# Two recurrent attention layers with streamed weights: at most three weight transfers under way, held back by a one-word read on SyncE

## The chip, the cores and the metric

The kernel runs on one core of a Trainium2 chip. The metric is the device time of one execution in microseconds, from the first to the last instruction. A core has five engines with a program each: TensorE (PE, matmuls; its weight loads are listed apart as PEld), VectorE (DVE), ScalarE (ACT), GpSimd (POOL) and SyncE (SP, which here only issues transfers). Sixteen DMA engines move data between device memory and the on-chip buffer. An engine waits for another one, or for a transfer, by a semaphore.

## The reference

Four layers follow each other, A B A B, each with a layer norm before it and a residual sum after it. The change touches layer A alone: attention over segments of 32 rows, each with 8 rows of memory that the segment before it has produced.

```python
# one A layer: x (2048, 640), 32 heads of 192, 64 segments of 32 rows, 8 memory rows
mem = mem0
for s in range(64):
    h = concat([mem, x[32*s : 32*s+32]])          # 40 rows
    q, k, v = h @ Wq, h @ Wk, h @ Wv              # 640 -> 32 x 192 = 6144 each
    p = softmax(where(mask, q k^T / sqrt(192), -1e9))
    o = (p v) @ Wo                                # 6144 -> 640
    mem = o[:8]                                   # the next segment needs it
    outs.append(o[8:])
```

Each segment needs the one before it, so the 64 segments of a layer are a chain, and each uses all four weight matrices. Layer B (a linear attention with softmax features) isn't touched.

## The kernel before

The four matrices of layer A are 31 MB together in bf16. Most of them stays in the on-chip buffer; the rest is loaded again in every segment. The heads are taken in four rounds r = 0, 1, 2, 3 of 8 heads, and every other segment goes through them backwards, so that the round that ends one segment begins the next. Rounds 1 and 2 are resident. Of rounds 0 and 3, which change places, 10 pieces of Wq, Wk and Wv (3 + 3 + 4 "slots" of 128 x 1536) and the four quarters of Wo's 128 x 7680 piece (`wo_end`) are streamed: as soon as TensorE has read a slot in the first round of a segment (n = 0), the piece of the last round (n = 3) is loaded into it.

```python
SLOTS = {"Q": 3, "K": 3, "V": 4}
...
def load_slot(m, r, b):                 # 128 x 1536 bf16 = 384 KB
    if holds.get((m, b)) != r:
        holds[m, b] = r
        nc.sync.dma_start(out=slot[m, b][:], in_=wview[m][:, b, PW * r:PW * r + PW])
...
def load_wo(r, into=None):              # four transfers of 480 KB
    t = into if into is not None else wo_end[:, :] if r in (0, 3) else wo_mid[:, 7680 * (r - 1):7680 * r]
    for k in range(4):
        nc.sync.dma_start(out=t[:, 1920 * k:1920 * k + 1920].rearrange("p (c m) -> p c m", m=640),
                          in_=wov[:, 12 * r + 3 * k:12 * r + 3 * k + 3, :])
```

The chain, cut to the order of its steps. The order of instructions on each engine is the order of the program here.

```python
def project(hT, ps, m, n, s, steps):
    ...
    for i in steps:
        b = (i + KC - ns) % KC if n == 0 else i      # round 0 of a segment reads the slots first
        w = piece(m, r, b)
        for g in range(4):
            ... nc.tensor.matmul(o[32 * g:32 * g + 32, 0:384], lhsT=hT[:, b, :], rhs=rhs, ...)   # L681
        if n == 0 and b >= KC - ns:
            load_slot(m, order[NR - 1], b)           # L522, on SyncE
...
for s in range(NSEG):
    for n, r in enumerate(order):
        ... project Q (with scores, softmax sums and normalisation of round 0 in between when n == 1)
        ... project K, project V
        if n > 0:
            O, OT = attend(E, n - 1)                 # L733
            extra_v(s, n + 1)                        # GpSimd: 2 x 14 KB, V of the segment's last 8 rows
        if n > 0:
            S, E = weigh()                           # L715, L722, L764
            wo_round(W, order[n - 1], OT, range(4), n == 1, False)        # L751
            sums(S, E)                               # L779
            wo_round(W, order[n - 1], OT, range(4, 12), n == 1, False)
            if n == 1:
                load_wo(order[NR - 1])               # L535, on SyncE: wo_end has been read
        ...
            next_kq(s, n)                            # GpSimd: copies K and Q of the segment's last 8 rows into
                                                     # place (L658 to L661), loads 96 KB of the next (kqb, L653)
    keep_busy(idle, 4)                               # matmuls whose result isn't used
    O, OT = attend(E, NR - 1)
    keep_busy(idle, 2)
    wo_round(W, order[NR - 1], OT, range(12), False, True)                # reads the new wo_end
    keep_busy(idle, 3)
    ... W -> wt -> hT[:, :, 0:8]                     # L866, L867: memory rows of the next segment
```

The chain projects the 8 memory rows and the first 24 rows of a segment; Q, K and V of its last 8 rows were computed before the chain and are read from device memory. In what follows a segment starts with the copy L867 (hT<-wt), with which its memory rows are complete.

The probes of the change use nothing of this but the order on SyncE, which has no other work in the chain.

Of the kernel before, what the change touches and what calls it, by code (L numbers as in the profile page):

```python
# [9 lines left out]
BF16 = mybir.dt.bfloat16  # L10
# [90 lines left out]
class Kernel:  # L101
# [389 lines left out]
    def layer_A(self, xn_dram, at_dram, li):  # L491
        nc, tc = self.nc, self.tc
        KC, NSEG = self.KC, self.NSEG
        dram = self.dram
        NR = 4
        PW = 1536
        self.kqb_d = dram.tile([NSEG, P, NR, 192], BF16, name=f"kqb{li}")
        self.vb_d = dram.tile([NSEG, NR, 2, 8, 896], BF16, name=f"vb{li}")
        self.otb_d = dram.tile([NSEG, P, 384], BF16, name=f"otb{li}")
        wview = self.wview  # L500
        wov = self.A_Wo.rearrange("h d m -> (h d) m").rearrange("(c p) m -> p c m", p=P)
        with tc.tile_pool(name=f"A{li}_wres", bufs=1) as wres:


            NRES = sum(KC - (SLOTS[m] if r in (0, 3) else 0) for m in "KQV" for r in range(NR))
            big = wres.tile([P, NRES * PW], BF16, name="w_res")
            res, at = {}, 0
            for r in (3, 0, 1, 2):
                for m in "KQV":
                    for b in range(KC - (SLOTS[m] if r in (0, 3) else 0)):  # L510
                        res[m, r, b] = big[:, at * PW:at * PW + PW]
                        at += 1
            slot = {(m, b): wres.tile([P, PW], BF16, name=f"wslot{m}{b}") for m in "KQV" for b in range(KC - SLOTS[m], KC)}
            holds = {}
            wo_mid = wres.tile([P, 24 * 640], BF16, name="wo_mid")
            wo_end = wres.tile([P, 12 * 640], BF16, name="wo_end")
            unread = set(res)

            def load_slot(m, r, b):
                if holds.get((m, b)) != r:  # L520
                    holds[m, b] = r
                    nc.sync.dma_start(out=slot[m, b][:], in_=wview[m][:, b, PW * r:PW * r + PW])  # L522

            def load_matrix(m, r):
                for b in range(KC):
                    if (m, r, b) in unread:
                        unread.remove((m, r, b))
                        nc.sync.dma_start(out=res[m, r, b], in_=wview[m][:, b, PW * r:PW * r + PW])
                    elif (m, r, b) not in res:
                        load_slot(m, r, b)  # L530

            def load_wo(r, into=None):
                t = into if into is not None else wo_end[:, :] if r in (0, 3) else wo_mid[:, 7680 * (r - 1):7680 * r]
                for k in range(4):
                    nc.sync.dma_start(out=t[:, 1920 * k:1920 * k + 1920].rearrange("p (c m) -> p c m", m=640),  # L535
                                      in_=wov[:, 12 * r + 3 * k:12 * r + 3 * k + 3, :])

            def piece(m, r, b):
                assert (m, r, b) in res or holds[m, b] == r
                return res[m, r, b] if (m, r, b) in res else slot[m, b]  # L540

            self.A_pre(xn_dram, li, load_matrix, piece, wo_mid, wo_end)
            self.A_chain(xn_dram, at_dram, li, load_slot, piece, load_wo, wo_mid, wo_end, big)
            self.A_post(at_dram, li, wo_mid, wo_end, big)

# [68 lines left out]
    def A_chain(self, xn_dram, at_dram, li, load_slot, piece, load_wo, wo_mid, wo_end, big):  # L614
        nc, tc, KC, NSEG = self.nc, self.tc, self.KC, self.NSEG
        scale = float(self.Dh) ** -0.5
        NR = 4
        with tc.tile_pool(name=f"A{li}_ch", bufs=1) as sp, \
# [16 lines left out]
            def rounds(s):  # L635
                return range(NR) if s % 2 == 0 else range(NR - 1, -1, -1)
# [31 lines left out]
            def project(hT, ps, m, n, s, steps):  # L668
                order = rounds(s)
                r = order[n]  # L670
                ns = SLOTS[m]
                for i in steps:
                    b = (i + KC - ns) % KC if n == 0 else i
                    w = piece(m, r, b)
                    for g in range(4):
                        if m == "V":
                            rhs = w[:, 384 * g:384 * g + 384]
                        else:
                            rhs = w[:, :].rearrange("p (c j) -> p c j", j=P)[:, :, 32 * g:32 * g + 32]
                        o = ps[g % 2] if m == "V" else ps  # L680
                        nc.tensor.matmul(o[32 * g:32 * g + 32, 0:384], lhsT=hT[:, b, :], rhs=rhs, start=(i == 0),  # L681
                                         stop=(i == KC - 1), tile_position=(0, 32 * g), skip_group_check=True)
                    if n == 0 and b >= KC - ns:
                        load_slot(m, order[NR - 1], b)

            def keys_or_queries(hT, m, n, s):
                ps = pqp.tile([P, 512], F32, name="ps_qk", tag="qk")
                project(hT, ps, m, n, s, range(KC))
                return ps
# [71 lines left out]
            def weigh():  # L761
                S = scores()
                E = sp.tile([P, 160], BF16, name="E", tag="E")
                nc.scalar.activation(out=E[:], in_=S[:, 0:160], func=ACT.Exp, scale=scale)  # L764
                return S, E
# [12 lines left out]
            def sums(S, E):  # L778
                nc.tensor.matmul(S[:, 256:416], lhsT=self.ones_blk[:, :], rhs=E[:, :], start=True, stop=True,  # L779
                                 skip_group_check=True)  # L780
# [18 lines left out]
            for s in range(NSEG):  # L799
# [3 lines left out]
                order = rounds(s)  # L803
                for n, r in enumerate(order):
                    pq = pqp.tile([P, 512], F32, name="ps_qk", tag="qk")
                    project(hT, pq, "Q", n, s, range(2))
                    if n == 1:
                        S, E = weigh()
                        next_kq(s, 0)
                    project(hT, pq, "Q", n, s, range(2, 4))  # L810
                    if n == 1:
                        sums(S, E)
                        normalise(S, E)
                    project(hT, pq, "Q", n, s, range(4, KC))
                    to_rows(pq, "Q")
                    pk = keys_or_queries(hT, "K", n, s)
                    to_rows(pk, "K")
                    if n == 0 and s > 0:
                        nc.gpsimd.dma_start(out=self.otb_d[s - 1], in_=otb[:, :, :, :].rearrange("p r c t -> p (r c t)"))
                        if s % 2 == 0:  # L820
                            store_rows(s - 2, ob_old)
                    pv = [pop.tile([P, 512], F32, name=f"ps_v{x}", tag=f"v{x}") for x in range(2)]
                    project(hT, pv, "V", n, s, range(3))
                    if n > 0:
                        O, OT = attend(E, n - 1)
                        if n + 1 < NR:
                            extra_v(s, n + 1)
                        elif s + 1 < NSEG:
                            extra_v(s + 1, 0)
                        if n == 1:  # L830
                            otb = sp.tile([P, NR, 12, 8], BF16, name="otb", tag="otb")
                        attend_rest(O, OT, otb, order[n - 1])
                    project(hT, pv, "V", n, s, range(3, KC))
                    if n > 0:
                        S, E = weigh()
                        wo_round(W, order[n - 1], OT, range(4), n == 1, False)
                        sums(S, E)
                        wo_round(W, order[n - 1], OT, range(4, 12), n == 1, False)
                        if n == 1:
                            load_wo(order[NR - 1])  # L840
                        if s == NSEG - 1 and n == 2:
                            load_wo(3, big[:, 0:7680])
                    v_rows(pv, n, 0, 0)
                    v_rows(pv, n, 1, 0)
                    v_rows(pv, n, 0, 1)
                    if n > 0:
                        normalise(S, E)
                    v_rows(pv, n, 1, 1)
                    if n > 0:
                        next_kq(s, n)  # L850
                    if n == NR - 1 and s + 1 < NSEG:
                        hT = hx_transpose(s + 1)
                        if s % 2 == 0 and s + 2 < NSEG:
                            load_rows(s + 2)
# [79 lines left out]
```

The softmax here doesn't subtract the row's maximum and nothing guards it: scores larger than these inputs give would overflow.

## Time and profile before

| what | value |
|---|---|
| time, median of 3 runs | 4346.16 us (4339.44 to 4354.84) |
| span of the profiled execution | 4350.8 us |
| TensorE busy | 3683.1 us, 85% |
| VectorE, ScalarE, GpSimd busy | 52%, 47%, 41% |
| mean granted TensorE clock | 0.948 |
| bytes moved | 983.28 MB, 226 GB/s over the span |
| of these by SyncE's and ScalarE's loads, q1 and q10 | 861.74 and 49.36 MB |
| q0 (transfers issued by GpSimd) | 60.56 MB |
| q8 and q14, "instruction" | 9.98 and 1.65 MB |

How to read it. The page gives the busy time of each engine, then the span in 40 slices with tenths of busy time, then the DMA queues, the chain of work that ended last, the costliest groups of instructions and the issues of transfers. Groups are written as line, engine, operation, tiles (out<-in), count. A wait is written as who waited, on which line, for whom: total us, how often, the longest. "Issue" stands for time in which an engine waited for nothing that the profile shows. Timeline rows begin with the start in us from the span's start and the length; rows of stretches give the length, then the busy time of PE, PEld, DVE, ACT and POOL with the number of instructions, the granted clock, the DMA share and GB/s. The page has two stretches of layer A's chain, at 272 to 1819 us and 2443 to 3976 us from the second segment on, two of layer B, and before each chain a short one in which the last 8 rows of every segment, whose projections don't depend on the chain, are projected for all segments at once.

### The profile page before, as it was taken

How to read it: one execution, taken by the hardware profiler on the slowest of the kernel's cores; microseconds unless marked ns; L12 is line 12 of the kernel's file. 1: busy time of each engine (PE TensorE's matmuls, PEld its weight loads, DVE VectorE, ACT ScalarE, POOL GpSimd, SP SyncE). 2: the span in 40 equal slices, each digit the busy share in tenths (PEclk: the TensorE clock that was granted, in tenths of full speed). 3: DMA queues.
4: the chain of work that ended last, by engine and by line, in shares of the span. 5: the costliest groups of instructions: out<-in, count | busy, mean ns of one | idle time of the engine just before them, and what ended most of it. 6: DMA issues, size and time to landing. Idle time of an engine off the chain costs nothing. (4 is left out here: it accounts for less than half of the span.)

```text
span 4350.8 us, 181511 instructions
## 1 busy us (share of the span) xinstructions
PE 3683.1 (85%) x77592; PEld 2223.0 (51%) x77608; DVE 2248.2 (52%) x5570; ACT 2024.4 (47%) x4973; POOL 1800.7 (41%) x5269
## 2 busy tenths in 40 slices
PE   5888888888888888869869888888888888888698
PEld 4645555555555555535347455555555555555353
DVE  4245555555555555536732455555555555554464
ACT  1245555555555555525412455555555555555152
POOL 1035555555555555430000355555555555553300
PEclk9989999999999999979989899999999999999798
DMA  7777777677677677740076876777777777777200
GB/s 258 214 264 271 254 274 259 247 268 257 247 261 262 239 275 258 273 126 1 31 248 193 280 269 240 273 259 258 276 250 271 251 262 271 252 266 272 84 1 25
DMA packets 613364, 983.28 MB, mean 226 GB/s; under 512 B 145098, under 2 KB 424650, under 8 KB 612554
## 3 DMA queue, kind: packets, MB, share of 16 engines
q1 hardware_dynamic: 459498, 861.74, 54.5%
q0 software_dynamic: 68224, 60.56, 4.6%
q10 hardware_dynamic: 84832, 49.36, 4.1%
q8 instruction: 609, 9.98, 0.9%
q14 instruction: 201, 1.65, 0.1%
HBM read 903.16 MB, written 68.16 MB: 223 GB/s over the span
## 5 line engine op out<-in xcount | busy, mean ns | idle before, releaser
L681 PEld LDWEIGHTS <-hT 128*32 128x32 bf16 x30720 | 785.9, 98 | 596.4 <-issue 217.7
L681 PE MATMUL ps_qk<-w_res,hT 128*32 128x384 bf16 x14336 | 804.8, 334 | 51.0 <-issue 48.0
L666 POOL DMA_DIRECT2D Vp<-vb x1024 | 539.1, 531 | 593.3 <-PE ps_o L733 518.5
L693 ACT ACTIVATE raw<-ps_qk 128x384 bf16<-128x384 f32 x1024 | 501.9, 490 | 547.4 <-PE ps_qk L681 529.4
L707 DVE CAST Vp<-ps_v 32x384 bf16<-32x384 f32 x1024 | 552.7, 540 | 36.3 <-PE ps_v L681 26.9
L751 PEld LDWEIGHTS <-OT 128*32 128x32 bf16 x24576 | 437.1, 99 | 234.0 <-issue 101.3
L698 DVE STREAM_TRANSPOSE QT<-raw 128x256 bf16<-128x256 bf16 x512 | 228.1, 445 | 613.9 <-ACT raw L693 604.1
L709 ACT ACTIVATE Vp<-ps_v 32x384 bf16<-32x384 f32 x1024 | 494.4, 483 | 64.0 <-PE ps_v L681 43.7
L658 POOL COPY QT<-kqb 128x64 bf16<-128x64 bf16 x512 | 121.8, 238 | 838.9 <-PE ps_s L722 403.5
L681 PE MATMUL ps_v<-w_res,hT 128*32 128x384 bf16 x6144 | 407.0, 330 | 29.7 <-issue 27.2
L786 DVE TENSOR_TENSOR E<-E,ps_s 128x160 bf16<-128x160 bf16 x512 | 164.6, 322 | 485.4 <-ACT ps_s L785 485.4
L751 PE MATMUL ps_w<-wo_mid,OT 128*32 128x160 bf16 x12288 | 351.1, 250 | 65.6 <-issue 63.0
L695 DVE STREAM_TRANSPOSE KT<-raw 128x384 bf16<-128x384 bf16 x512 | 296.1, 578 | 71.8 <-ACT raw L693 57.3
L739 ACT ACTIVATE OT<-ps_o 128x240 bf16<-128x240 f32 x512 | 190.0, 371 | 287.8 <-PE ps_o L733 275.7
L764 ACT ACTIVATE E<-ps_s 128x160 bf16<-128x160 f32 x512 | 155.7, 304 | 360.8 <-PE ps_s L722 356.6
L751 PE MATMUL ps_w<-wo_end,OT 128*32 128x160 bf16 x12288 | 290.5, 235 | 30.2 <-issue 15.9
L722 PE MATMUL ps_s<-QT,KT 128*40 128x40 bf16 (+1 forms) x6144 | 183.4, 189 | 127.9 <-DVE KT L695 63.3
L758 PE MATMUL ps_idle<-wo_mid,ident 128*128 128x384 bf16 x1152 | 270.0, 346 | 0.0
L681 PE MATMUL ps_v<-wslotV,hT 128*32 128x384 bf16 x4096 | 249.6, 332 | 22.8 <-issue 20.7
L743 DVE CAST OT<-ps_o 128x240 bf16<-128x240 f32 x512 | 195.9, 383 | 126.6 <-PE ps_o L733 122.9
L745 POOL COPY otb<-OT 128x48 bf16<-128x48 bf16 x1024 | 198.4, 231 | 125.1 <-ACT OT L739 117.3
L653 POOL DMA_DIRECT2D kqb<-kqb x256 | 148.0, 578 | 232.5 <-DMA vb<-wo_end 153.9
(148 smaller groups left out, 5485.4 us busy)
## 6 DMA issues: line engine op xcount, KB each, us to landing
wo_end<-in_A_Wo_dram SPq DMA_DIRECT2D x520, 480.0 KB
wslotV<-in_A_Wv_dram SPq DMA_DIRECT2D x536, 384.0 KB
wslotK<-in_A_Wk_dram SPq DMA_DIRECT2D x402, 384.0 KB
wslotQ<-in_A_Wq_dram SPq DMA_DIRECT2D x402, 384.0 KB
kqb<-wo_mid ACTq DMA_DIRECT2D x16, 1536.0 KB
kqb<-kqb POOLq DMA_DIRECT2D x256, 96.0 KB, 5.5
Vp<-vb POOLq DMA_DIRECT2D x1024, 14.0 KB, 4.8
vb<-wo_end ACTq DMA_DIRECT2D x128, 112.0 KB
```

Of the source, the lines that this page charges most:

```text
L666: nc.gpsimd.dma_start(out=Vs[n % 2][64 * G + 32:64 * G + 40, :], in_=self.vb_d[s, r, G])
L681: nc.tensor.matmul(o[32 * g:32 * g + 32, 0:384], lhsT=hT[:, b, :], rhs=rhs, start=(i == 0), stop=(i == KC - 1), tile_position=(0, 32 * g), ...
L693: nc.scalar.activation(out=raw[:], in_=ps[:, 0:384], func=ACT.Copy)
L695: nc.vector.transpose(out=KT[:, :, 0:32], in_=raw[:, :].rearrange("p (c j) -> p c j", j=32))
L698: nc.vector.transpose(out=qv[:, :, 0:4:3, 8:40], in_=rv[:, :, 0:3:2, :])
L707: nc.vector.tensor_copy(out=o, in_=i)
L709: nc.scalar.activation(out=o, in_=i, func=ACT.Copy)
L739: nc.scalar.activation(out=OT[0].rearrange("p c q -> p (c q)"), in_=O[0][:, 0:240], func=ACT.Copy)
L743: nc.vector.tensor_copy(out=OT[1].rearrange("p c q -> p (c q)"), in_=O[1][:, 0:240])
L745: nc.gpsimd.tensor_copy(out=otb[:, r, 6 * G:6 * G + 6, :], in_=OT[G][:, :, 0:8])
L751: nc.tensor.matmul(W[32 * g:32 * g + 32, 0:160], lhsT=OT[c // 6][:, c % 6, 8:40], rhs=w[:, 640 * c + 160 * g:640 * c + 160 * g + 160], sta ...
L758: nc.tensor.matmul(ps[:, 0:384], lhsT=self.ident[:, :], rhs=wo_mid[:, 0:384], start=True, stop=True, skip_group_check=True)
```

## The change

Layer A gets a pacing of the streamed weights. `flying` lists the last loads. Before a fourth one, SyncE issues a probe: a transfer of one word (two bf16 values) out of the buffer that the third last load fills, into a scratch tensor in device memory. The probe reads what that load writes, so it has to wait until the load has landed, and since SyncE issues in order, the next load stands behind it. So no more than three streamed loads are under way. It is meant to keep the DMA queues short, so that other users of the DMA engines wait less. The ten slots and the four quarters of `wo_end` in each segment are paced; the loads before the chain and one of the last segment into `w_res` are not. The scratch tensor has 16 rows, used in turn.

```diff
+            probe = dram.tile([16, 2], BF16, name=f"probe{li}")
+            flying = []
+            probes = [0]
+
+            def pace(ap):
+                if len(flying) == 3:
+                    nc.sync.dma_start(out=probe[probes[0] % 16:probes[0] % 16 + 1, :], in_=flying.pop(0)[0:1, 0:2])
+                    probes[0] += 1
+                flying.append(ap)
+
-            def load_slot(m, r, b):
+            def load_slot(m, r, b, paced=False):
                 if holds.get((m, b)) != r:
                     holds[m, b] = r
+                    if paced:
+                        pace(slot[m, b])
                     nc.sync.dma_start(out=slot[m, b][:], in_=wview[m][:, b, PW * r:PW * r + PW])
...
-            def load_wo(r, into=None):
+            def load_wo(r, into=None, paced=False):
                 t = into if into is not None else wo_end[:, :] if r in (0, 3) else wo_mid[:, 7680 * (r - 1):7680 * r]
                 for k in range(4):
+                    if paced:
+                        pace(t[:, 1920 * k:1920 * k + 1920])
                     nc.sync.dma_start(out=t[:, 1920 * k:1920 * k + 1920].rearrange("p (c m) -> p c m", m=640),
...
-                        load_slot(m, order[NR - 1], b)
+                        load_slot(m, order[NR - 1], b, True)
...
-                            load_wo(order[NR - 1])
+                            load_wo(order[NR - 1], None, True)
```

A transfer that is issued on SyncE takes one of eight semaphores in turn, and each has to be free again. In the changed program loads and probes alternate, so a probe also waits for the probe four before it.

## The prediction

> **What bounds the kernel now.** I read the page from the top: shares of busy time, the 40 slices, the DMA queues. The two "A" layers fill most of the span (slices 2 to 17 and 22 to 37), and in them TensorE is at 8 tenths and the DMA at 7, with no engine full:
>
> ```profile
> PE 3683.1 (85%) x77592; PEld 2223.0 (51%) x77608; DVE 2248.2 (52%) x5570; ACT 2024.4 (47%) x4973; POOL 1800.7 (41%) x5269
> ...
> PE   5888888888888888869869888888888888888698
> ...
> q1 hardware_dynamic: 459498, 861.74, 54.5%
> ...
> q8 instruction: 609, 9.98, 0.9%
> ```
>
> Two lines carry what follows. q1 holds the weight stream. q8 is TensorE's own program: 77592 + 77608 = 155200 instructions in 609 packets are 255 for each packet, and 9.98 MB / 155200 is 64 bytes each.
>
> So I asked what TensorE's matmuls wait for in the chain of the first A layer (272.6 to 1819.4 us, 62 whole segments). The waits, in us, times and the longest:
>
> ```profile
> PE ps_qk L681 <- issue: 43.0, 35, 2.2
> PE ps_w L751 <- issue: 37.8, 32, 1.7
> PE ps_s L722 <- DVE KT L695: 30.0, 124, 0.3
> PE ps_v L681 <- issue: 25.6, 17, 2.2
> PE ps_o L733 <- issue: 14.1, 11, 2.2
> PE ps_s L722 <- POOL KT L661: 13.9, 19, 2.8
> PE ps_s L722 <- issue: 9.3, 8, 1.5
> ```
>
> "Issue" means that no semaphore held it. With two waits of L715 (4.1) that is 133.9 us here and 122.7 us in the other chain: **257 us** in which TensorE has data and no instruction. The timeline of TensorE shows one such wait, and the one before it:
>
> ```profile
> 879.24 0.73 PE L751 MATMUL ps_w<-wo_mid,OT 128*32 128x160 bf16 x31 [0.80 <-issue]
> ...
> 883.36 0.32 PE L751 MATMUL ps_w<-wo_mid,OT 128*32 128x160 bf16 x7
> 885.32 0.37 PE L751 MATMUL ps_w<-wo_mid,OT 128*32 128x160 bf16 x9 [1.64 <-issue]
> ```
>
> Between the two starts lie 127 matmuls and 128 weight loads, 255 instructions: one packet of q8. The packet itself ran at 883.09, 3.85 us after 879.24, and TensorE went on 2.23 us after its start. In the trace 215 of the packets in the two chains are followed by such a stop, 270 us together, restart at a median 2.38 us after the packet's start. All of them lie 6 to 20 us after a segment's start. The stretches of one segment say why:
>
> ```profile
> 841.30:845.30 4.00, 3.74 (x90) 2.22 (x89) 2.30 (x7) 2.31 (x6) 0.78 (x2) 1.00 0.70 205
> ...
> 849.30:853.30 4.00, 3.61 (x105) 2.18 (x101) 1.89 (x6) 2.52 (x6) 1.09 (x4) 1.00 1.03 400
> 853.30:857.30 4.00, 3.01 (x98) 1.90 (x91) 2.05 (x5) 2.20 (x6) 3.03 (x12) 1.00 1.05 383
> ...
> 861.30:865.10 3.80, 3.71 (x106) 2.25 (x105) 1.63 (x5) 1.76 (x5) 3.02 (x10) 1.00 0.10 16
> ```
>
> The last two columns are DMA share and GB/s. The DMA is full from about 845 to 859 and empty at the end; TensorE's busy time (first column after the length) is worst where it is full. From the first use of a block to the start of the next block's packet the trace has a median of 1.1 us at 20 to 22 us of a segment (empty queue) and 3.7 to 3.8 us at 10 to 14 us (about 5 to 6 us of stream queued). Blocks take 4.4 to 5.3 us to execute; a delay plus 2.4 us above that is a stop. So the limit to stay under is a delay of about 2.0 to 2.4 us.
>
> **What the Trainium skill says.** "Runtime: NRT & Kernel Launch", section "Instruction fetch mechanics", says that a sequencer fetches its program over a DMA queue of its own, in 16 KiB blocks of 256 instructions, mostly hidden. The block size agrees (9.98 MB / 609); hidden it is not here. "DMA: Bandwidth & Descriptors", section "Queues, rings and completion order", has each DMA engine go round between queues by packets; a fetch thus does not wait for the whole backlog, which agrees with a delay that stops growing at 3.8 us. The section "Anatomy of one DMA" of that page puts some 2 us of fixed time on a transfer, mostly the receipt. The trace agrees: the segment's first load is issued at 841.92 and its first engine reports at 844.66, 2.74 us, of which 1.05 us is movement (393 KB at 375 GB/s). "TensorE: Matmul & The Clock Gate", Part 1, says that an idle window puts the array to half clock for about 3.4 us. The trace has such stretches in 51 of 124 whole segments, mostly beside a stop of over 1 us; those segments last 25.70 us on average, the others 24.24.
>
> **The change, part by part.** There are 128 segments, on average 24.84 us. Each streams 10 slots of 393 KB and 4 pieces of Wo of 491 KB, 5.9 MB.
>
> *Adds:* 14 probes a segment, one descriptor of 4 bytes each, behind two loads at most. SyncE's small stores (attn<-obB) take 0.26 us each; 14 x 0.26 = 3.7 us of SyncE in 24.8, which has only these loads to do. Nothing is added on TensorE, VectorE, ScalarE or GpSimd.
>
> *Takes away:* the backlog. Now all ten slots are issued within 5.3 us of the first (0.63 to 5.9 us into a segment, medians of the trace) and Wo follows at 8.0 to 10.7. With three under way, of which one is always being set up or waiting for its receipt (2.74 - 1.05 = 1.7 us), one to one and a half transfers stand in the queue, 1.0 to 1.6 us. The empty-queue delay of 1.1 us plus this is 2.1 to 2.7 us at worst and mostly below 2.4. I take it that four fifths of the 257 us go: 205 us. With the long stops go some of the half-clock stretches: 51 x (25.70 - 24.24) = 74 us, of which I count half, 37. The wait for the kqb rows (POOL KT L661, 13.9 + 11.9 = 26 us) shrinks for the same reason; half is 13. Sum: **255 us**, 2.0 us a segment.
>
> *Moves:* the arrivals, later. The loop is: third-last landing, probe, load, landing. That is 2.74 us, some 0.45 us for another packet on the slowest engine, 0.26 us probe and 0.2 us of gaps: 3.65 us for three, 1.22 us for each slot. Wo pieces take 0.27 us longer to move and issue in 0.4 to 1.2 us instead of 0.38: about 4.4 us for three, 1.47 each. From the first landing at 4.2 us: 4.2 + 9 x 1.22 + 4 x 1.47 = 21.1 us for the last Wo piece, against 20.1 now (median). Its reader, the last wo_round, starts at 22.4 us in the segment of the timeline (863.65 - 841.3). But without 2.0 us of stops it starts at 20.4, and its last quarter runs at 21.1. The stream and TensorE then come out about equal, and what scatters adds: I take half a microsecond a segment of new waits for Wo, 128 x 0.5 = 64 us. The V slots (tenth landing at 15.2 against a use at about 16.6) are just in time.
>
> Net: 255 - 64 = 191 us, and 4346 - 191 = **4155**; I write 4160.
>
> **Rivals.** *The stream becomes the bound.* For it: the slots have 1.4 us of room and Wo none; a 0.95 us program packet on one engine delays the landing that releases the next load, where now the queue hides it. If the pitch is 1.35 and 1.65 us, the last piece lands at 23 us, a segment is 23.8 us (0.8 us from landing to the next segment's start) and only 1 us x 128 = 130 us remain: 4215. At 1.5 and 1.8 us nothing remains: 4350. *The fetch delay does not depend on depth.* If one queued transfer holds a fetch as long as five, nothing is gained and the later stream costs: 4350 to 4400. Against it: in the trace the delay grows with what is queued, 1.1 us at nothing, 1.9 us at about 2 us of stream, 3.7 us above 4 us. *All goes*: fetches, half clock and kqb together, 357 us, and the stream keeps pace: 3990. *The probe's store itself is slow*: each probe waits also for the probe four before it, so if a store takes over 4 x 1.2 us to land, it sets the pitch.
>
> **Range and chances.** The centre is the sum above. 4040 is nearly everything without new waits; 4300 is the stream bound with a pitch of about 1.45 us. Two per cent is 4259, which needs less than half of the 191 us to be there; the mechanism is seen in the trace, only the pitch is guessed. I give 0.79 to faster, 0.16 to within 2%, 0.05 to slower.
>
> **What would show it.** Waits on "issue" before matmuls down from 257 us to some 50; half-clock stretches in the chains rarer; DMA share in the middle of a segment at 0.8 to 0.95 instead of 1.03, and loads spread to 18 us or more after a segment's start; kqb to landing below 5.5 us. New: TensorE waits on DMA wo_end and on the V slots, together below 100 us. Layers B and the stretches before the chains must not change. I am wrong if "issue" stays above 150 us, or if the waits on wo_end exceed 150 us.

## The result and the profile after

The changed kernel took **4550.97 us** (median of 4 runs, 4540.87 to 4566.98) against 4348.05 us for the kernel before on the same chips: a ratio of **1.0471** (95% interval 1.0435 to 1.0507). It is slower by 203 us, where some 190 us less had been expected.

The page of the kernel after, lines as shown of the kernel before, and from its fourth part the shares of the chain that ended last, by engine and by line:

```profile
PE 3784.6 (83%) x77592; PEld 2223.9 (49%) x77608; DVE 2252.5 (50%) x5570; ACT 2024.4 (45%) x4973; POOL 1798.4 (40%) x5269
...
PE   5978888888888888868869788888888888887698
...
q1 hardware_dynamic: 463070, 861.75, 58.4%
...
q8 instruction: 609, 9.98, 0.9%
...
PE 30%; DMA 26%; DVE 6%; ACT 5%; issue 3%; SPq 1%; POOL 1%; ACTq 0%; POOLq 0%; DVEq 0%
DMA wo_end<-in_A_Wo_dram 16%; PE ps_qk L696 7%; DMA wslotV<-in_A_Wv_dram 6%; PE ps_w L766 4%; PE ps_v L696 2%; PE ps_qk L342 2%; PE pp L906 2%; PE ps_pre L608 2%; DVE KT L710 2%; DMA wslotK<-in_A_Wk_dram 2%; PE ps_s L737 2%; PE ps_wo L455 1%; ACT raw L708 1%; DVE QT L713 1%; PE ps_idle L773 1%
```

Same program on TensorE (77592 matmuls, 609 packets on q8), 101.5 us more of busy time for it. Same bytes on q1 (861.75 MB), and its packets take a larger share of a longer span: 58.4% of 4539 us against 54.5% of 4351 us, 280 us more on each of the 16 engines. The chain that ended last could be followed back over 72% of the span; 16% of the span in it is the landing of `wo_end` and 6% that of V slots. The chain of the kernel before could be followed over 16% of its span only, so the two can't be compared as shares; neither of these two loads is among its pieces.

What TensorE waits for in the chain of the first A layer (from the second segment on, 278.9 to 1918.2 us: 1639 us instead of 1547):

```profile
PE ps_w L766 <- DMA wo_end<-in_A_Wo_dram: 132.6, 117, 3.0
PE ps_v L696 <- DMA wslotV<-in_A_Wv_dram: 48.6, 45, 2.8
...
PE ps_w L766 <- issue: 3.7, 6, 1.0
PE ps_o L748 <- issue: 2.0, 2, 1.2
...
PE ps_v L696 <- issue: 1.4, 2, 1.1
PE ps_s L737 <- POOL KT L676: 1.0, 1, 1.0
```

The stops on "issue" are gone as intended: 22 us before matmuls of both chains instead of 264. They are not just hidden under the new waits: of stops whose program packet runs 6 to 14 us into a segment, where TensorE doesn't wait for weights in either kernel, 11 us of 140 are left. In their place stand waits for streamed weights: 264 us for `wo_end` and 104 us for the V slots, over both layers (5 and 2 us before).

One segment of 26.21 us, in stretches of 4 us. Columns: length, busy time of PE, PEld, DVE, ACT and POOL with instructions, granted clock, DMA share, GB/s:

```profile
1229.10:1233.10 4.00, 4.00 (x46) 1.70 (x48) 1.12 (x4) 0.79 (x2) 0.00 (x0) 0.50 0.46 135
...
1237.10:1241.10 4.00, 3.69 (x122) 2.33 (x118) 2.95 (x8) 2.59 (x7) 1.43 (x4) 1.00 0.86 282
1241.10:1245.10 4.00, 3.91 (x126) 2.47 (x122) 2.81 (x7) 2.60 (x7) 2.85 (x12) 1.00 0.90 290
1245.10:1249.10 4.00, 3.92 (x110) 2.24 (x106) 2.92 (x8) 2.51 (x7) 2.15 (x6) 1.00 0.87 253
1249.10:1253.10 4.00, 3.15 (x90) 1.84 (x91) 1.21 (x4) 1.65 (x5) 1.91 (x9) 1.00 0.88 288
```

The DMA moves 250 to 290 GB/s in the middle, where it moved 380 to 400 before. That is 0.71 of the rate, while the DMA share falls only to 0.84 of what it was (from about 1.04 to 0.88): the engines are partly idle, and the same bytes also take them longer (see the last section). The first stretch shows the clock at 0.50: 46 matmuls fill all four microseconds. The end of the segment, in the timeline of TensorE:

```profile
1251.34 0.60 PE L766 MATMUL ps_w<-wo_end,OT 128*32 128x160 bf16 x24
1252.34 0.39 PE L766 MATMUL ps_w<-wo_end,OT 128*32 128x160 bf16 x12 [0.40 <-DMA wo_end<-in_A_Wo_dram]
1254.28 0.59 PE L766 MATMUL ps_w<-wo_end,OT 128*32 128x160 bf16 x12 [1.55 <-DMA wo_end<-in_A_Wo_dram]
1254.80 1.14 PE L773 MATMUL ps_idle<-wo_mid,ident 128*128 128x384 bf16 x3
```

TensorE is done with all else and waits for the third and the fourth quarter of Wo. The last one landed 25.14 us after the segment's start, and the segment ended 1.07 us later.

The stream, in medians over the 124 whole segments of the two chains (us from a segment's start; a landing is the report of the last of 16 DMA engines):

| | before | after |
|---|---|---|
| tenth slot lands | 14.85 | 17.97 |
| last quarter of Wo lands | 20.09 | 25.17 |
| from landing to landing, slots / Wo | 1.19 / 1.30 | 1.52 / 1.79 |
| from a load's issue to the first engine's report, fourth slot on | 4.5 to 7.4 | 2.8 to 3.6 |
| from the first engine's report to the last one's | 0.73, rising to 2.11 | 0.60, rising to 1.64 |
| mean segment | 24.84 | 26.22 |

124 x (26.22 - 24.84) = 171 us of the 188 us between the two profiled spans lie in these segments.

### The profile page after: what moved, and what is told of

It reads as the page before. It is cut to its first block, busy times and chain, and to the rows that moved or that the text cites. A ratio compares the mean times of both kernels' runs of the same rounds, so it can differ in the third digit from the quotient of the medians.

```text
span 4539.2 us, 183299 instructions
## 1 busy us (share of the span) xinstructions
PE 3784.6 (83%) x77592; PEld 2223.9 (49%) x77608; DVE 2252.5 (50%) x5570; ACT 2024.4 (45%) x4973; POOL 1798.4 (40%) x5269
## 3 DMA queue, kind: packets, MB, share of 16 engines
q1 hardware_dynamic: 463070, 861.75, 58.4%
## 4 chain that ended last, share of the span: by engine, by line
PE 30%; DMA 26%; DVE 6%; ACT 5%; issue 3%; SPq 1%; POOL 1%; ACTq 0%; POOLq 0%; DVEq 0%
DMA wo_end<-in_A_Wo_dram 16%; PE ps_qk L696 7%; DMA wslotV<-in_A_Wv_dram 6%; PE ps_w L766 4%; PE ps_v L696 2%; PE ps_qk L342 2%; PE pp L906 2%; PE ps_pre L608 2%; DVE KT L710 2%; DMA wslotK<-in_A_Wk_dram 2%; PE ps_s L737 2%; PE ps_wo L455 1%; ACT raw L708 1%; DVE QT L713 1%; PE ps_idle L773 1%
## 5 line engine op out<-in xcount | busy, mean ns | idle before, releaser
L766 PE MATMUL ps_w<-wo_end,OT 128*32 128x160 bf16 x12288 | 345.3, 240 | 278.2 <-DMA wo_end<-in_A_Wo_dram 263.8
L696 PE MATMUL ps_v<-w_res,hT 128*32 128x384 bf16 x6144 | 390.0, 329 | 4.6 <-issue 4.5
L696 PE MATMUL ps_v<-wslotV,hT 128*32 128x384 bf16 x4096 | 264.0, 341 | 107.2 <-DMA wslotV<-in_A_Wv_dram 104.0
L766 PE MATMUL ps_w<-wo_mid,OT 128*32 128x160 bf16 x12288 | 324.5, 242 | 3.4 <-issue 2.7
L773 PE MATMUL ps_idle<-wo_mid,ident 128*128 128x384 bf16 x1152 | 296.6, 373 | 0.0
L883 ACT ACTIVATE ob<-ps_w 128x160 bf16<-128x160 f32 x128 | 38.9, 304 | 514.6 <-DVE wt L881 426.7
L881 DVE STREAM_TRANSPOSE wt<-ps_w 128x160 f32<-128x160 f32 x126 | 44.1, 350 | 447.2 <-PE ps_w L766 447.2
```

Source lines behind the costliest of these rows:

```text
L766: nc.tensor.matmul(W[32 * g:32 * g + 32, 0:160], lhsT=OT[c // 6][:, c % 6, 8:40], rhs=w[:, 640 * c + 160 * g:640 * c + 160 * g + 160], sta ...
L773: nc.tensor.matmul(ps[:, 0:384], lhsT=self.ident[:, :], rhs=wo_mid[:, 0:384], start=True, stop=True, skip_group_check=True)
```

## The experiments

Two theories. **Too few:** three loads under way are not enough to cover a load's way from issue to landing, with a probe or without. **The probe:** three would do, and the probe's store is what costs: it holds up a DMA engine, or SyncE.

### Three under way without a probe

Both kernels below hold a load by a semaphore on the third last load. The first has no probe at all, the second issues after each load a probe that reads a constant and gates nothing.

```diff
-    if len(flying) == 3: <probe of flying.pop(0)>
+    d = nc.sync.dma_start(<the load>)
+    if len(flying) == 3: <d waits for the landing of flying.pop(0)>
+    flying.append(d)
```

> Three loads under way as in the change, but without the probe: the load itself waits for the landing of the third last one. Theory S (the probe holds up the DMA engine that carries it, about 0.5 us each, so that this engine's part of every load comes late): from one landing to the next 1.25 us for slots and 1.5 us for Wo instead of 1.52 and 1.79, the last Wo quarter lands at about 21 us after the segment's start instead of 25.2, a segment is 22 to 23 us, the time 4050 to 4150 us. Theory L (three under way are too few whatever holds them back): only the probe's 0.3 us of each loop is saved, 1.42 and 1.69 us, last landing at 23.7 us, a segment 24.6 us, the time about 4340 us.

> As e1, with a probe after each load that holds back nothing: it reads one word of the constant identity matrix and writes it to the same scratch tensor in device memory. Theory S: landings 1.45 us or more apart again, the time 4450 to 4550 us. Theory L: as e1 within 30 us.

Measured: 4447.62 us (ratio 1.0244, 1.0211 to 1.0277) and 4472.87 us (1.0293, 1.0260 to 1.0326). Waits of TensorE in the kernel without probes:

```profile
PE ps_w L774 <- DMA wo_end<-in_A_Wo_dram: 243.6, 242, 2.7
PE ps_v L704 <- DMA wslotV<-in_A_Wv_dram: 47.3, 61, 2.1
...
PE ps_w L774 <- issue: 9.7, 12, 2.0
PE ps_o L756 <- issue: 6.5, 9, 1.3
```

With no probe in the program the waits on `wo_end` are nearly those of the change. The slots land every 1.43 us and the Wo quarters every 1.80 (theory L had 1.42 and 1.69, and a time of 4340 us that proved 108 us too low); from issue to landing a slot takes 3.8 to 4.6 us from the third on, and the last engine reports up to 1.8 us after the first. So three loads are too few by themselves (+101 us against 4346), and the probe's store isn't what makes an engine late. As traffic the probe costs 25 us at most or nothing: the two intervals overlap. Between its absence and its place in the loop lie 103 us (4551 against 4448).

### A slower probe

The change, with the probe writing into an on-chip tile instead of device memory:

```diff
-    probe = dram.tile([16, 2], ...)
+    probe = wres.tile([P, 32], ...)
```

> The change with its probes writing to a scratch tile in the on-chip buffer instead of device memory. If the store to device memory is what holds up the engine (theory S): landings 1.3 to 1.35 us apart, the time 4150 to 4300 us. If any probe does, or under theory L: 4500 to 4560 us.

Measured: 4719.25 us (1.0861, 1.0818 to 1.0904), slower than either theory had it. SyncE's timeline, first of the change, then of this kernel (start, length, what is issued):

```profile
1239.92 0.24 SPq L526 DMA_DIRECT2D probe<-wslotK  x1
1240.21 0.33 SPq L535 DMA_DIRECT2D wslotV<-in_A_Wv_dram  x1
```

```profile
1230.51 0.59 SPq L526 DMA_DIRECT2D probe<-wslotK  x1
1231.13 0.40 SPq L535 DMA_DIRECT2D wslotV<-in_A_Wv_dram  x1
```

The issue of this probe takes 0.59 us instead of 0.24, and both stand between a landing and the next load. From the landing on, the probe puts the next load off by nothing (no probe), 0.29 and 0.62 us in the three kernels; they take 4448, 4551 and 4719 us, and a slot lands every 1.43, 1.52 and 1.65 us. A third of 0.29 and of 0.62 us, added to 1.43, is 1.53 and 1.64: one loop carries three loads, and what these probes add to it shows in the pitch.

### How many under way

The kernel without probes, with 4, 5 and 6 in place of 3, and the change itself with one digit altered (`len(flying) == 4`):

> As e1 with four loads under way. Theory S: three were enough, so the time is that of e1 within 50 us, a little more waiting for instructions. Theory L: the loop of 4.3 us carries four loads instead of three, landings about 1.15 us apart, 150 us or more faster than e1, 4150 to 4200 us.

> As e4 (4252.7 us) with five loads under way. Theory L: the stream no longer binds, waits of TensorE on Wo and the V slots under 15 us, last Wo landing at about 21 us; but more is queued in front of TensorE's program packets, its waits on issue rise from 145 to about 200 us; the time 4230 to 4290 us, at or a little above e4.

> With six under way: nearly the kernel before. Waits on issue 230 us or more, the time 4290 to 4340 us. If the delay of a program packet doesn't grow with what is queued, e4, e5 and e6 wait alike, and e6 is as fast as e4 or faster.

> The change itself with four instead of three in its list. Theory L: the probe's 0.3 us in each loop costs less than with three (loop of 5.5 us over four loads: 0.07 us a load, 1 us at the last landing), partly hidden behind waits that e4 had anyway; the time 4290 to 4360 us, near the kernel before and some 200 us faster than the change.

In the table, "landing to landing" is that of slots and Wo quarters; stops, waits and half clock are totals of the trace (us: stops on issue before matmuls of the chain, waits on `wo_end` and V slots, length of the stretches in the chains at less than full clock).

| under way | time, ratio (interval) | landing to landing | stops | Wo + V | half clock |
|---|---|---|---|---|---|
| 3 and probe (the change) | 4550.97, 1.0471 (1.0435 to 1.0507) | 1.52 / 1.79 | 22 | 368 | 393 |
| 3 | 4447.62, 1.0244 (1.0211 to 1.0277) | 1.43 / 1.80 | 24 | 291 | 304 |
| 4 and probe | 4288.62, 0.9884 (0.9848 to 0.9920) | 1.31 / 1.71 | 124 | 93 | 157 |
| 4 | **4252.71, 0.9780 (0.9743 to 0.9816)** | 1.24 / 1.70 | 145 | 50 | 157 |
| 5 | 4286.55, 0.9878 (0.9841 to 0.9915) | 1.19 / 1.40 | 207 | 10 | 130 |
| 6 | 4319.45, 0.9944 (0.9920 to 0.9967) | 1.18 / 1.32 | 245 | 9 | 160 |
| before: no pacing | 4343 to 4350 | 1.19 / 1.30 | 264 | 7 | 191 |

The waits of TensorE with four under way:

```profile
PE ps_w L774 <- issue: 82.5, 86, 2.7
...
PE ps_w L774 <- DMA wo_end<-in_A_Wo_dram: 44.2, 57, 2.4
...
PE ps_o L756 <- issue: 24.6, 25, 1.9
...
PE ps_v L704 <- DMA wslotV<-in_A_Wv_dram: 5.9, 8, 1.7
```

The two costs run against each other, as "too few" has it: each further load under way gives fetch stops back and, up to five, takes waits for weights away. From five on the slots land no sooner (every 1.19, 1.18 and 1.19 us); a load only takes longer, for the tenth slot 5.8, 6.9 and 9.1 us from issue to landing. Four gained less than theory L had it (4150 to 4200 us, landings 1.15 us apart); five, six and "4 and probe" came out in their ranges or within 2 us of them. At four the sum is least: **4253 us beats both kernels**, and the change with one digit altered is faster than the kernel before, too. Half clock doesn't follow the stops alone: it is least at five, and longest where TensorE waits for Wo at the end of a segment.

### Bytes or transfers

Is it the number of transfers under way or the data in them? First each load in halves by partitions (0 to 63, 64 to 127), six halves under way:

> Each load in two halves by partitions (64 + 64, the same row lengths), six halves under way: as many bytes as in e1, twice as many transfers. If bytes under way set the pace (theory L): as e1, 4400 to 4470 us, or somewhat faster since a half is released earlier. If the number of transfers under way set it (a fixed time for each one that overlaps): as e6, 4290 to 4340 us.

Measured: 5020.92 us (1.1566, 1.1528 to 1.1604). This is no answer to the question: the packets themselves slow down. A packet of a slot (3072 bytes) takes 176 ns in the median instead of 121, one of Wo (1280 bytes) 81 instead of 55. Over 121 and 55 ns that is 17223 us together (over all engines), against 6418 us with three whole loads. So the slots were halved by columns instead (128 x 768, rows of 1536 bytes), a quarter of Wo counting as two halves, six under way:

```diff
-    d = nc.sync.dma_start(out=slot[m, b][:], in_=...)          # hold(d): 3 loads
+    for i in (0, 768):
+        d = nc.sync.dma_start(out=slot[m, b][:, i:i + 768], in_=...)   # hold(d): 6 halves
```

> No probes. Each slot goes out as two transfers of half its columns (128 x 768, rows of 1536 bytes), six such halves may be under way; a quarter of Wo counts as two. So the bytes under way are those of e1_hold3 (4447 us: pitch of a slot 1.43 us, waits on wo_end 244 us), the number of slot transfers is that of e6_hold6 (4319 us: pitch 1.18 us, waits on wo_end 7 us). Theory bytes (what counts is the data under way): 4405 to 4460 us, a slot every 1.35 to 1.45 us. Theory count (what counts is how many transfers are in the pipeline of issue, movement and receipt): 4310 to 4350 us, a slot every 1.18 to 1.25 us. Between the two: both play a part; the next half goes out when a half has landed instead of a whole slot, which is worth up to a quarter of a pitch.

Measured: 4505.40 us (1.0378, 1.0349 to 1.0408), above what either theory gave and on the side of the bytes. TensorE's waits:

```profile
PE ps_w L777 <- DMA wo_end<-in_A_Wo_dram: 249.0, 241, 3.1
...
PE ps_v L707 <- DMA wslotV<-in_A_Wv_dram: 50.3, 68, 2.2
```

A slot (two halves) lands every 1.50 us, although the number of transfers is that of the kernel with six whole loads and 1.18 us. In the trace a half takes 4.0 to 4.4 us from issue to landing from the eighth on (2.3 to 2.8 us to the first engine's report, 1.2 to 1.8 from there to the last one's), no less than a whole slot. At the same bytes under way this time is the same for halves and for whole slots, so the pace is the bytes under way divided by it: 3 x 393 KB / 4.3 us = 275 GB/s, within the 250 to 290 of the stretches. Why the halves are 58 us slower than whole slots was not tried; one thing seen is that two rows of 1536 bytes usually take 2 x 65 ns, one of 3072 bytes 121.

### Parts of the change alone

The change's probes on the slots only, and on the quarters of Wo only:

> The change with its probes on the ten slots alone; Wo goes out freely. The slots arrive as in the change (the tenth at about 18.0 us), Wo follows at its own rate of 1.3 us, the last at about 23 us instead of 25.2: 2 us less at the end of a segment, but the waits on the V slots (104 us) stay. 4330 to 4420 us.

> The change with its probes on the four Wo quarters alone; the list then holds Wo quarters only, so at most one of a segment's four is held. The slots run as before. Nearly the kernel before: 4330 to 4370 us.

Measured: 4485.51 us (1.0317, 1.0290 to 1.0343) and 4286.48 us (0.9868, 0.9841 to 0.9895). Both expectations missed. With slots alone, the slots land as late as in the change (the tenth at 18.20 us), and the unpaced Wo stands behind them on SyncE and comes at 24.61: V slots cost 171 us, Wo 140. So it is the pacing of the ten slots that does the harm; freeing the quarters gives back only a third of it. With Wo alone the kernel is *faster* than before, for a reason that I hadn't seen. SyncE's timeline:

```profile
1230.04 0.24 SPq L526 DMA_DIRECT2D probe<-wo_end  x1
1231.06 0.38 SPq L550 DMA_DIRECT2D wo_end<-in_A_Wo_dram  x1
1231.95 0.24 SPq L526 DMA_DIRECT2D probe<-wo_end  x1
1236.26 0.38 SPq L550 DMA_DIRECT2D wo_end<-in_A_Wo_dram  x1
1236.69 0.33 SPq L526 DMA_DIRECT2D probe<-wo_end  x1
```

The probe ahead of the first load reads a word of the second quarter, the third last load then. The second load overwrites that word, so it waits until this probe has landed: it starts 6.2 us after the probe's issue. By that time the probe's store had the slots' backlog before it. Thus the second quarter goes out at a median of 13.7 us of a segment instead of 8.6, when most slots have landed, and still the last one lands at 22.00, just in time (12.5 us of waits). The slots, unpaced, land as before; stops go from 264 to 209 us and half clock from 191 to 102. That the load waits for the probe's landing follows from the program. That the backlog delays the probe shows in the landings: the four probes of a segment take a median of 6.5, 5.5, 2.8 and 3.1 us to land, the first two behind the slots.

### GpSimd's loads as the cause of the late engine

Three under way without a probe, and without GpSimd's loads of kqb and V rows inside the chain. It leaves out part of the computation: K, Q and V of the last 8 rows of a segment are not brought up to date.

> e1 (4447.6 us) without GpSimd's loads of the K, Q and V rows (kqb and Vp) inside the chain, so the attention uses rows of the first segment for those 8 rows; the output is not the reference's. If these 250 KB a segment are what makes the slowest DMA engine late (1.3 to 1.7 us behind the first), the lag falls below 1 us, landings come 1.25 us apart, and the time is 4150 to 4250 us. If not, the lag stays at 1.2 us or more and the time is 4370 to 4440 us.

Measured: 4341.53 us (0.9979, 0.9967 to 0.9991), 106 us less than with these loads and below the range that was given for "if not"; whether it is their bandwidth or GpSimd's own time for them is not separated. But the lag from the first to the last engine stays at 1.3 to 1.7 us, a slot lands every 1.37 us, and the waits for Wo stay:

```profile
PE ps_w L775 <- DMA wo_end<-in_A_Wo_dram: 208.2, 199, 3.1
PE ps_v L705 <- DMA wslotV<-in_A_Wv_dram: 32.1, 48, 1.6
```

They are not what makes an engine late.

### Two depths in one kernel

If the slots set the stops and Wo the waits, four slots and five quarters should beat four of both; the mirror is five slots and four quarters:

> As e4, but a Wo quarter may be the fifth under way. In e4 TensorE still waits 44 us for Wo, in e5 8 us. If both halves of the trade are right, those 36 us go and the waits on issue (145 in e4) grow by less than that: 4225 to 4265 us. If the Wo transfers are what the program packets of the third round stand behind, issue grows by 50 us and the time is that of e5, about 4285.

> No probes; a slot may be the fifth transfer under way, a quarter of Wo only the fourth (the mirror of e9_slots4_wo5, which took 4339 us, while four of both took 4253 and five of both 4287). Theory W (a fifth quarter of Wo is what costs, because it lies in the DMA queues while TensorE's program is fetched in the second half of the segment): 4240 to 4275 us, stops on issue 130 to 170 us in the kernel. Theory D (depth of the slots sets the stops, the quarters do not matter): about as five of both, 4275 to 4300 us, stops about 200 us. If it is above 4310 us, neither: then mixing two depths itself costs, and I have no explanation for it.

Measured: 4339.31 us (0.9982, 0.9963 to 1.0001) and 4317.50 us (0.9922, 0.9894 to 0.9949). Both missed: each mix is slower than four of both (4253) and five of both (4287). The stops in the trace, summed by the time in the segment at which the program packet runs:

| under way, slots and Wo | 6 to 14 us | from 14 us on | waits for Wo |
|---|---|---|---|
| 4 and 4 | 34 | 111 | 44 |
| 5 and 5 | 108 | 104 | 8 |
| 5 and 4 | 97 | 134 | 11 |
| 4 and 5 | 51 | 179 | 18 |

The fifth slot costs 63 to 74 us in the first part, in both rows that have it. The 65 us by which five and four end above four and four are mostly this. The fifth quarter, after four slots, costs 68 us of stops at 14 us and later and half-clock stretches of 246 us instead of 157; after five slots it costs nothing there. Five and five has its last quarter in at 20.6 us, four and five at 22.2, so more of its program packets run beside the stream; whether that is all of it stays open.

## Why the prediction was wrong

- **What bounds the kernel:** right, and the *takes away* step too. The stops on issue went from 264 to 22 us (expected: to about 50), the wait for the kqb rows from 26 to 1 us (expected: half), and kqb (GpSimd's load) lands in a median 4.3 us instead of 5.5. Shorter queues do let the program through.
- **Half clock:** the sign was wrong. 37 us fewer were counted on; the half-clock stretches grew from 51 with 191 us together to 98 with 393 us. At the same count of matmuls TensorE was busy 101.5 us longer. The trace shows the wait for Wo at the end of a segment ahead of the half clock of the next (67 of the 98 begin later than 24 us into a segment or in its first microsecond; before, none did): removing one kind of idle time and adding another cancels this gain.
- **Moves: the step that failed.** Of the loop of 3.65 us, the 2.74 us to the first engine were right for slots (2.8 to 3.1 measured; 3.2 to 3.6 for quarters of Wo), so was the probe (0.24), but for the slowest engine I took 0.45 us; it is 1.4 us on average for the fourth to the tenth slot (medians 1.1 to 1.6) and 1.6 for a quarter of Wo. About 0.95 us more in a loop of three is 0.3 us for each slot: 1.22 + 0.3 = 1.52, as measured; the loop takes 4.6 us, not 3.65. From there the prediction's own formula gives the rest: 4.2 + 9 x 1.52 + 4 x 1.79 = 25.0 us for the last quarter (25.17 measured), 4 us past its use. A warning was to be had beforehand: the trace of the kernel before has this lag at 0.73 us for a segment's first load, and at 1.1 to 2.1 us from the third on, though behind a longer queue. The section that the prediction cites for some 2 us of fixed time is about transfers that GpSimd issues; the loop rests on the trace's own 2.74 us for SyncE's.
- **Waits for weights:** 64 us counted, 368 us measured, mostly from that one term. With the 101.5 us of busy time this outweighs the roughly 267 us that the stops and kqb gave: 361 + 101 - 267 = 195, against 188 between the two spans.
- **The rivals.** "The stream becomes the bound" is what happened, at the pitches of its worst line (1.5 and 1.8 us). But that line's 4350 us didn't follow from its own rule: 4.2 + 9 x 1.5 + 4 x 1.8 = 24.9, and 0.8 more is a segment of 25.7 us, 0.86 us above the 24.84 of before, or 4346 + 110 = 4456 us. The range's upper end of 4300 at 1.45 us has the same slip (about 4370, with 1.75 us for Wo). Worked out rightly, the rival would have shown that the change could lose 110 us where it was said to break even. "The fetch delay doesn't depend on depth" fell with the table of depths. "The probe's store itself is slow" fell with the trace: it lands 2.5 us after its issue in the median, well under the 4 x 1.2 us that would have set the pitch. What counts is the probe's time between a landing and the next load. The prediction's limit for the fetch delay, 2.0 to 2.4 us, should read 2.0 to 2.9 by its own figures (4.4 to 5.3 less 2.4); nothing in the result hangs on it.
- **Signs named beforehand:** DMA share of 0.8 to 0.95 came true (0.86 to 0.90), and so did the sign of error, waits on `wo_end` above 150 us.

Open is which DMA engine is late and why, and why packets take longer behind a shorter queue. It isn't the probe (without it the lag is 1.1 to 1.8 us) and not GpSimd's rows; the trace doesn't tell the engines of a transfer apart, so a program packet or slow packets of one engine were not tried as causes.

## What to carry to other kernels

A tight limit on transfers under way is a bandwidth limit: bytes under way divided by the sum of the time from issue to the *last* engine's landing and whatever stands between that landing and the next issue. Take the lag of the last engine from loads in the middle of the stream, not from the first one into an empty queue (1.1 to 2.1 us here against 0.73), and compare the resulting landings with the first use before anything is paced. The whole time from issue to landing can't be read from an unpaced stream, where it is mostly queue (5.6 to 9.1 us here from the fourth load on). Then scan the depth: here three, four and six differ by up to 195 us, and the best lies one step from the worst.

## What had not been expected of the hardware

- Behind a shorter queue more packets take long. The usual one keeps its 121 ns (row of a slot) or 55 ns (row of Wo) with whole loads at every depth, but of 181760 slot packets 7286 take 200 ns or more with no pacing, 10189 with four under way, 14683 with three and 15696 in the change. The time over 121 and 55 ns, summed over all engines, is 2579 us with no pacing, 2640 with six under way, 3455 with five, 4735 with four, 6418 with three and 6983 in the change.
- A one-word store issued on SyncE takes 0.24 us of SyncE when it goes to device memory and 0.59 us when it goes to the on-chip buffer.
- Loads of 64 partitions instead of 128, the bytes under way being the same, cost 573 us (5021 against 4448), with 2.7 times as much packet time above the 121 and 55 ns.
